# RetNet and SwiGLU on one core: the heads of a pair change places on the partitions in odd chunks, and VectorE's order around a slot changes

## The chip, the cores and the metric

The kernel runs on one core of one Trainium2 chip. The metric is the device time of one execution in microseconds; the time before is a median of three runs. All arithmetic is in fp32.

## The reference

Two parts follow one another. The first is retention in its parallel form, for 8 batches, 8 heads, 576 positions and a head size of 64. The second is a gated feed-forward layer (4608 tokens, model size 512, inner size 1536) on the result:

```python
scores = scale * np.matmul(q, k.transpose(0, 1, 3, 2))       # scale = 1/8
gamma = 1.0 - 2.0 ** (-5.0 - np.arange(H))
Dmat = np.where(rel >= 0, gamma[:, None, None] ** rel[None, :, :], 0.0)   # rel = row - column
attn = np.matmul(scores * Dmat[None], v)
x = attn.transpose(0, 2, 1, 3).reshape(B * S, H * D)
...
rms = np.sqrt(np.mean(x * x, axis=-1, keepdims=True) + 1e-06)
xn = x / rms * rms_g
g = xn @ w_gate
out = (g / (1 + np.exp(-g)) * (xn @ w_val)) @ w_out
```

## The kernel before

**Retention by chunks.** A job is one batch and one pair of heads: 32 jobs, four to a batch, so job j belongs to batch j // 4. The 576 positions are 9 chunks of 64. Within a chunk the kernel multiplies scores by a causal mask and by v; what earlier chunks contribute comes through a 64 x 64 state per head, the decayed sum of k-transposed times v over the chunks before. Row decays are folded into v ahead and into x at the end (the table gq).

The work of a job is spread over two slots, and `slot(j)` does these things in this order:

- `values(j - 1)` (L332): masked scores times v, into two PSUM banks, `av[0]` for even and `av[1]` for odd chunks.
- `scores(j)` (L270) and `states(j)` (L290): scores and chunk states of the next job, into the three banks `s` and one bank `last`.
- `weigh(j)`, on VectorE: two products `ret` (scores times mask, L303), and then the eight running sums of states (a copy at L313 and seven fused multiply-adds at L315, each of which needs the one before). The last sum reads the bank `last`.
- `carried(j - 1)`: 16 matmuls (L351) add the states' part to `av`, and four VectorE products (L366) move `av`, times gq, to `x`.

All these matmuls are 64 x 64 x 64. Each uses one quadrant of the array: the row half comes from the partitions of its inputs, the column half from those of its output. The two heads e = 0, 1 of a pair lie on partitions 0 to 63 and 64 to 127, in the inputs of `carried` (`sum`, `qT`) and in x alike; `side(e)` is that slice. A fp32 matmul leaves two records in the trace, so `carried` shows 32.

Before `carried` writes over what `values` wrote from another row half, a small GpSimd memset (`tick`, L340) that waits for `values` holds it back.

**The feed-forward layer.** A unit u is 384 tokens, 12 units. Units 0 and 1 run plainly (L536, L550), with the preparation of the weights beside them. From unit 2 on every product is made as a Strassen-like product of seven block products. `up(u, m, g)` makes one group: seven products (L479) in the order x, y, z, x, w, z, w, each 8 records on TensorE, into the banks x, y, z, w. m = 0 is the gate and m = 1 the value; three g each, so six groups i = 0 to 5 per unit. VectorE adds partial results: u2 = m1 + y and u4 = u2 + z (L486), after which the second z product may write into the bank z; results follow at L486 and L496. `across(u)` then makes the output product, again seven products of 24 records (L609), in the order x, z, w, y, x, z, w.

**The order.** It is written out by hand (`manual_schedule`): the order of the calls is the order of each engine's queue. `SLOTS` says behind which groups of a unit a slot runs. Units with u % 3 == 2 have slots behind groups 1, 3 and 5, those with u % 3 == 0 behind 0, 2, 4 and 5, those with u % 3 == 1 behind 5. So slots 10 to 12 lie in unit 2, 13 to 16 in unit 3, 17 in unit 4, and so on to slot 32 in unit 9; slots 0 to 9 are in `start()`. Of slots 9 to 32, eight (12, 16, 17, 20, 24, 25, 28, 32) are followed by `across`, the others by another group. Behind slot j follow on VectorE the transposes of q and k for the next job (L241). In unit 2 one add of w_out (`combine_out`, L580) is put between the products, as long as there are any.

The norm of the next unit is spread too: squares on ScalarE (L404) and their sums on VectorE (L410) behind group 5 (`norm_0`); the mean over the model size by three small matmuls `ms` (L422), a power on GpSimd (L428) and the diagonals (L435) behind the second product of `across` (`norm_1`); and the broadcast `rb` (L446) with the scaling of x (L448) behind the fifth (`norm_2`).

PSUM has eight banks: three for `s`, and five that serve everything else in turn; a bank is given out again once its last reader has finished.

Of the kernel before, what the change touches and what calls it, by code (L numbers as in the profile page):

```python
# [10 lines left out]
F32 = mybir.dt.float32  # L11
U32 = mybir.dt.uint32
AF = mybir.ActivationFunctionType
ALU = mybir.AluOpType
P = 128
L = P // 2


def _gamma(H):
    return 1.0 - 2.0 ** (-5.0 - np.arange(H, dtype=np.float64))  # L20


def _decay_tables(H, D):


    pairs = _gamma(H).reshape(H // 2, 2).T
    rows = np.repeat(pairs, D, axis=0)
    pos = np.arange(L)
    p = np.concatenate([pos, pos])
    t = (  # L30
        pairs.T[None] ** -p[:, None, None], rows**L,
        rows[:, :, None] ** (pos + L) / np.sqrt(D),
    )
    return [np.ascontiguousarray(x).astype(np.float32) for x in t]


def _causal_table():

    return np.ascontiguousarray(np.tile(np.triu(np.ones((L, L), np.float32)), (2, 1)))
# [3 lines left out]
def kernel(  # L43
# [11 lines left out]
    nc = tc.nc  # L55
    B, H, S, D = q.shape
    NTOK, DM = out.shape
    DFF = moe_w_gate.shape[1]
    NHP = H // 2
# [10 lines left out]
    NG = NH // 2  # L70
# [5 lines left out]
    const = ctx.enter_context(tc.tile_pool(name="const", bufs=1))  # L76
# [11 lines left out]
    def bank(name):  # L88
        return banks.tile([P, 512], F32, tag="b", name=name)
# [15 lines left out]
    top = cell("top", 255.0 * 2.0**23)  # L105
    causal = const.tile([P, L], F32, name="causal")
    gq = const.tile([P, NHP, L], F32, name="gq")
    gv = const.tile([P, NHP, 2], F32, name="gv")
    gc = const.tile([P, NHP], F32, name="gc")
    tick = const.tile([1, 1], F32, name="tick")  # L110
# [16 lines left out]
    jobs = [(b, hp) for b in range(B) for hp in range(NHP)]  # L127
    st = [{} for _ in jobs]
# [128 lines left out]
    def side(i):  # L257
        return slice(i * L, i * L + L)
# [16 lines left out]
    def state_of(d, c):  # L275

        i, odd = divmod(c, 2)
        if odd and SC + i * L == 512:
            return d["last"][:, :L]
        return d["s"][:, 1, SC + i * L : SC + i * L + L] if odd else d["s"][:, 2, i * L : i * L + L]  # L280
# [13 lines left out]

    def weigh(j):


        d = st[j]
        hp = jobs[j][1]
        s = d["s"]  # L300
        ret = d["ret"] = att.tile([P, 2, NFULL + 1, L], F32, tag="ret", name=f"ret_{j}", bufs=1)
        for e in range(2):
            nc.vector.scalar_tensor_tensor(  # L303
                out=ret[:, e], in0=s[:, e, :SC].rearrange("p (c k) -> p c k", k=L),
                scalar=float(_gamma(H)[2 * hp + e] ** -L),
                in1=causal.unsqueeze(1).to_broadcast([P, NFULL + 1, L]),
                op0=ALU.mult, op1=ALU.mult,
            )
        t = d["sum"] = att.tile([P, NC - 1, L], F32, tag="sum", name=f"sum_{j}")
        for c in range(NC - 1):  # L310
            part = state_of(d, c)
            if c == 0:
                nc.vector.tensor_copy(out=t[:, 0], in_=part)  # L313
                continue
            nc.vector.scalar_tensor_tensor(  # L315
                out=t[:, c], in0=t[:, c - 1], scalar=gc[:, hp : hp + 1], in1=part,
                op0=ALU.mult, op1=ALU.add,
            )
        del d["s"], d["last"]

    def follow(a, b):
        why = mybir.DependencyInfo(mybir.DependencyClass.Sync, mybir.DependencyReason.DATA)
        tc.add_manual_dep(a.ins, b.ins.name, why, reason="rows of the array")

    def values(j):

        d = st[j]
        av = d["av"] = [bank(f"av_{j}_{i}") for i in range(2)]
        for c in range(NC):
            i, odd = divmod(c, 2)  # L330
            for e in range(2):
                mm = nc.tensor.matmul(  # L332
                    av[odd][side(e), i * L : i * L + L],
                    lhsT=d["v"][side(odd), i, e] if c < NC - 1 else d["vt"][:, e],
                    rhs=d["ret"][side(odd), e, i],
                    start=(c < 2), stop=False, skip_group_check=True,
                )


        d["valued"] = nc.gpsimd.memset(tick, 0.0)  # L340
        follow(d["valued"], mm)

    def carried(j):

        d = st[j]
        b, hp = jobs[j]
        av = d["av"]
        for c in range(1, NC):
            i, odd = divmod(c, 2)
            for e in range(2):  # L350
                mm = nc.tensor.matmul(  # L351
                    av[odd][side(e), i * L : i * L + L], lhsT=d["sum"][side(e), c - 1],
                    rhs=d["qT"][side(e), c * L : c * L + L],
                    start=False, stop=(c >= NC - 2), skip_group_check=True,
                )
                if c == 1 and e == 0:
                    follow(mm, d["valued"])
        for c0, c1 in ((0, 2 * HU), (2 * HU, S)) if b % 2 == 0 else ((0, HU), (HU, S)):
            u, o = divmod(b * S + c0, U)
            if u not in x_of:  # L360
                x_of[u] = xp.tile([P, NHP, U], F32, tag="x", name=f"x_{u}")
            x = x_of[u][:, hp, o : o + c1 - c0].rearrange("p (c k) -> p c k", k=L)
            for first in (c0 // L, c0 // L + 1):
                i, odd = divmod(first, 2)
                n = -(-(c1 // L - first) // 2)
                nc.vector.tensor_tensor(  # L366
                    out=x[:, first - c0 // L :: 2],
                    in0=av[odd][:, i * L : (i + n) * L].rearrange("p (c k) -> p c k", k=L),
                    in1=gq[:, hp].unsqueeze(1).to_broadcast([P, n, L]), op=ALU.mult,
                )  # L370
        st[j] = {}

    def slot(j, rest=True):

        if j > len(jobs):
            return
        if rest and j > 0:
            values(j - 1)
        if j < len(jobs):
            scores(j)  # L380
            states(j)
        if j < len(jobs):
            weigh(j)
        if rest and j > 0:
            carried(j - 1)

    def prepare_next(j):
        if j + 1 < len(jobs):
            prepare(j + 1)

    def load_next(j):
        if j + 2 < len(jobs):
            load_qk(j + 2)
            load_kv(j + 2)
# [283 lines left out]
    for g in range(NG):  # L678
        for m, src in enumerate((moe_w_gate, moe_w_val)):
            for half in range(2):  # L680
                n = (half * NH + 2 * g) * P
# [13 lines left out]
    def spare(i):  # L695

        return i % 4 if i < n_up else LATER[i - n_up]
# [15 lines left out]
    def load_chunks(n, queue=nc.scalar):  # L713

        nonlocal n_loads
        while n_loads < min(n, len(chunks)) and waits_at.get(spare(n_loads)) is None:
            load_chunk(n_loads, queue)
            n_loads += 1
# [94 lines left out]
    def start():  # L813

        h_of[0] = ffn.tile([P, NF, U], F32, tag="h", name="h_0")
        tables = list(zip((causal, gv, gc, gq), (_causal_table(), *_decay_tables(H, D))))

        def table(i, queue):
            t, values_ = tables[i]
# [9 lines left out]
        for j in range(2 * NHP):  # L829
            load_first(j)  # L830
            if j == 0:
                load_tails(0, (nc.scalar, nc.scalar, nc.sync))
            elif j == 1:
                table(3, nc.sync)
            elif j == 3:
                load_tails(1, (nc.sync,) * 3)
            load_chunks((0, 0, 1, 1, 2, 2, 2, 3)[j], nc.sync)
        nc.sync.dma_start(out=rms_g, in_=moe_rms_g.rearrange("(c p) -> p c", p=P))
        load_chunks(4, nc.sync)
        turn(0)  # L840
# [3 lines left out]
        for j in range(2 * NHP):  # L844
# [7 lines left out]
            if j:  # L852
                u, c = divmod(j - 1, NHP)
# [34 lines left out]
        for u in (1, 0):  # L888
# [6 lines left out]
            if u:  # L895
                combine(1)
                slot(8, rest=False)
                following(8)
        slot(9)
        following(9)  # L900

    SLOTS = (((0, 2, 4, 5), 5), ((5,), 9), ((1, 3, 5), 10))
# [14 lines left out]
    with tc.manual_schedule():  # L919
        start()  # L920
        for u in range(2, NU):
            made = combine_out() if u == 2 else iter(())
            for i in range(2 * NG):
                for _ in up(u, i % 2, i // 2):
                    next(made, None)
                if u > 2 and i in (1, 3):
                    fetch()
                    fetch()
                if i == 2 * NG - 1:
                    rest = across(u)  # L930
                    next(rest)
                behind(u, i)
            for i, _ in enumerate(rest):
                if i == 1:
                    behind(u, 6)
                elif i == 2 and 2 * NG - 1 in SLOTS[u % 3][0]:
                    at, n = SLOTS[u % 3]
                    load_next(u // 3 * 8 + n + len(at) - 1)
                elif i == 4:
                    behind(u, 7)  # L940

# [26 lines left out]
```

## Time and profile before

| | |
|---|---|
| time, median of three runs | 1184.26 us (1182.89 to 1184.86) |
| profiled span | 1180.2 us |
| TensorE busy, matmul | 1144.4 us, 97% |
| VectorE busy | 671.1 us, 57% |
| ScalarE busy | 248.2 us, 21% |
| carried matmuls, L351 | 1024 records, 38.2 us busy |
| x products, L366 | 128 instructions, 35.5 us in all |
| sums of states, L315 | 224 instructions, 62.8 us in all |

A line of the groups by form gives source line, engine, operation, out<-in by name, the shape and the count; then the busy time, the mean of one in ns, and the idle time ahead of the group with what ended it. A line of the timeline gives start, duration, and instruction; several of a kind are merged, with their count. PEld is the weight load ahead of a matmul, and it carries the matmul's waits. Matmul records on different quadrants overlap, so their number times their duration is not their share of the span.

### The profile page before, as it was taken

What the parts mean: (1) busy time and instruction counts of PE and PEld (TensorE: products, weight loads), DVE (VectorE), ACT (ScalarE), POOL (GpSimd) and SP (SyncE); (2) the same over time, 40 slices, a digit from 0 to 9 for tenths busy, and PEclk for the clock granted to TensorE, in tenths of its full rate; (3) what the DMA queues carried; (4) which work ended last, traced back from release to release, by engine and by line L of the source; (5) the groups of instructions that cost most, each with busy time, mean ns of one, the idle gap of its engine ahead of it and who ended that gap; (6) DMA issues with size and microseconds to landing.
All of it is one profiled execution on the core that took longest, in us unless ns stands there. A gap on an engine that the chain in (4) does not pass through costs nothing.

```text
span 1180.2 us, 24260 instructions
## 1 busy us (share of the span) xinstructions
PE 1144.4 (97%) x10320; PEld 1037.0 (88%) x10320; DVE 671.1 (57%) x1362; ACT 248.2 (21%) x484; POOL 46.8 (4%) x74
## 2 busy tenths in 40 slices
PE   6789999999999999999999999999999999999998
PEld 5655555448999999999999999999999999999998
DVE  4688874118666574455664665465566555536442
ACT  5445641111211221111121120120220210120110
POOL 0000005400000000000000000000000000000000
PEclk9899999999999999999999999999999999999999
DMA  9744312322954536126335446306525502403304
GB/s 223 205 112 146 139 72 58 125 66 41 264 134 66 164 96 138 62 72 122 101 94 94 110 117 137 117 17 123 132 64 133 157 5 85 130 1 94 121 1 108
DMA packets 282220, 125.24 MB, mean 106 GB/s; under 512 B 257152, under 2 KB 264704, under 8 KB 282112
## 3 DMA queue, kind: packets, MB, share of 16 engines
q1 hardware_dynamic: 271440, 108.32, 36.4%
q10 hardware_dynamic: 10672, 15.38, 3.9%
q8 instruction: 81, 1.33, 0.5%
q14 instruction: 27, 0.22, 0.1%
HBM read 108.70 MB, written 14.94 MB: 105 GB/s over the span
## 4 chain that ended last, share of the span: by engine, by line
PE 85%; DVE 10%; DMA 2%; ACT 2%; issue 1%; SPq 0%; DVEq 0%; POOL 0%; POOLq 0%; ACTq 0%
PE x L479 13%; PE z L479 13%; PE w L479 13%; PE up L536 8%; PE wo L609 7%; PE y L479 7%; PE out L550 5%; PE xo L609 4%; PE zo L609 4%; PE yo L609 3%; DVE sum L315 2%; PE av L351 2%; PE av L332 1%; PE s L270 1%; DVE sq L410 1%
## 5 line engine op out<-in xcount | busy, mean ns | idle before, releaser
L503 ACT COPY m<-x 128x384 f32<-128x384 f32 x60 | 28.7, 478 | 430.9 <-PE x L479 430.9
L479 PE MATMUL z<-x,w_gate 128*128 128x192 f32 x480 | 87.9, 326 | 2.2 <-DVE sum L315 2.2
L479 PE MATMUL x<-x,w_val 128*128 128x192 f32 x480 | 89.8, 331 | 0.0
L479 PE MATMUL x<-x,w_gate 128*128 128x192 f32 x480 | 88.6, 328 | 0.0
L479 PE MATMUL w<-sums,w_gate 128*128 128x192 f32 x480 | 87.8, 326 | 0.0
L479 PE MATMUL z<-x,w_val 128*128 128x192 f32 x480 | 87.8, 326 | 0.0
L479 PE MATMUL w<-sums,w_val 128*128 128x192 f32 x480 | 87.8, 326 | 0.0
L609 PE MATMUL xo<-h,w_out 128*128 128x192 f32 x480 | 82.1, 328 | 0.0
L609 PE MATMUL wo<-h,w_out 128*128 128x192 f32 x480 | 82.0, 328 | 0.0
L479 PEld LDWEIGHTS z<-x,w_gate 128*128 128x128 f32 x480 | 79.6, 190 | 2.5 <-DVE sum L315 2.5
L479 PEld LDWEIGHTS x<-x,w_val 128*128 128x128 f32 x480 | 80.0, 192 | 0.6
L479 PEld LDWEIGHTS x<-x,w_gate 128*128 128x128 f32 x480 | 79.3, 190 | 0.5
L479 PEld LDWEIGHTS w<-sums,w_val 128*128 128x128 f32 x480 | 79.7, 190 | 0.0
L479 PEld LDWEIGHTS w<-sums,w_gate 128*128 128x128 f32 x480 | 79.7, 190 | 0.0
L479 PEld LDWEIGHTS z<-x,w_val 128*128 128x128 f32 x480 | 79.6, 190 | 0.0
L609 PEld LDWEIGHTS xo<-h,w_out 128*128 128x128 f32 x480 | 78.1, 190 | 0.5
L609 PEld LDWEIGHTS wo<-h,w_out 128*128 128x128 f32 x480 | 78.1, 190 | 0.0
L486 DVE TENSOR_TENSOR u<-m,y 128x384 f32<-128x384 f32 x60 | 32.8, 546 | 79.4 <-PE y L479 79.4
L486 DVE TENSOR_TENSOR h<-u,w 128x384 f32<-128x384 f32 x60 | 33.3, 555 | 73.7 <-PE w L479 73.7
L303 DVE SCALAR_TENSOR_TENSOR ret<-s,causal 128x320 f32<-128x320 f32 x64 | 28.4, 485 | 67.0 <-PE last L290 42.2
L498 ACT ACTIVATE h<-h 128x384 f32<-128x384 f32 x90 | 47.0, 523 | 88.6 <-DVE h L486 88.6
L536 PE MATMUL up<-x,w_val 128*128 128x384 f32 x192 | 62.7, 487 | 2.1 <-ACT w_val L544 2.1
(150 smaller groups left out, 1783.0 us busy)
## 6 DMA issues: line engine op xcount, KB each, us to landing
w_out<-w_blocks SPq DMA_DIRECT2D x70, 768.0 KB, 5.1
out_dram<-o SPq DMA_DIRECT2D x304, 24.0 KB, 1.6
qraw<-in_q_dram SPq DMA_DIRECT2D x96, 72.0 KB, 2.6
kraw<-in_k_dram SPq DMA_DIRECT2D x96, 72.0 KB, 2.6
k<-in_k_dram SPq DMA_DIRECT2D x48, 128.0 KB, 2.9
v<-in_v_dram SPq DMA_DIRECT2D x48, 128.0 KB, 2.8
w_blocks<-w_out SPq DMA_DIRECT2D x7, 768.0 KB, 7.0
w_out<-in_moe_w_gate_dram ACTq DMA_DIRECT2D x4, 1024.0 KB, 5.2
```

The lines of the kernel that those rows point to most:

```text
L270: nc.tensor.matmul(s[side(odd), e, i * L : i * L + L], lhsT=d["kT"][side(e), c * L : c * L + L], rhs=d["qT"][side(e), c * L : c * L + L], ...
L303: nc.vector.scalar_tensor_tensor(out=ret[:, e], in0=s[:, e, :SC].rearrange("p (c k) -> p c k", k=L), scalar=float(_gamma(H)[2 * hp + e] ** ...
L315: nc.vector.scalar_tensor_tensor(out=t[:, c], in0=t[:, c - 1], scalar=gc[:, hp : hp + 1], in1=part, op0=ALU.mult, op1=ALU.add,)
L332: mm = nc.tensor.matmul(av[odd][side(e), i * L : i * L + L], lhsT=d["v"][side(odd), i, e] if c < NC - 1 else d["vt"][:, e], rhs=d["ret"][s ...
L351: mm = nc.tensor.matmul(av[odd][side(e), i * L : i * L + L], lhsT=d["sum"][side(e), c - 1], rhs=d["qT"][side(e), c * L : c * L + L], start ...
L479: nc.tensor.matmul(ps[:, i * HU : i * HU + HU], lhsT=w_up[m][:, 2 * blk + c, cut], rhs=t_of[u][blk][:, c], start=(start and i == c == 0), ...
L486: nc.vector.tensor_tensor(out=o, in0=a, in1=pairs_of(ps), op=ALU.add)
L498: nc.scalar.activation(out=o, in_=c, func=AF.Silu)
L503: nc.scalar.copy(out=s1, in_=pairs_of(x_))
L536: nc.tensor.matmul(ps[:, :U], lhsT=w_up[m][:, 4 * half + c, i * P : i * P + P], rhs=x_of[u][:, c], start=(c == 0), stop=(c == NHP - 1),)
L550: nc.tensor.matmul(ps[:, :DM], lhsT=h_of[u][:, f, s * P : s * P + P], rhs=w_out[:, f], start=(f == 0), stop=(f == NF - 1),)
L609: nc.tensor.matmul(ps[:, i * HU : i * HU + HU], lhsT=w_slots[:, k % 4, c, i * P : i * P + P], rhs=rhs[:, c], start=(start and i == c == 0) ...
```

## The change

It has three parts.

1. *Exchange.* From job 8 on, the products of odd chunks write head e to the other half of the partitions, in `values` and in `carried`. In `carried`, even chunks then use two quadrants of the array and odd chunks the other two. The last VectorE products bring the heads back to their places: each product of an odd chunk becomes two of 64 partitions, which read one half and write the other. They need the decay table with its halves exchanged, gx, which is loaded ahead of rms_g.
2. *x ahead of the sums.* The sums of states leave `weigh` and become `sums(j)`. From slot 8 on they run after `carried(j - 1)`, so the x products come first on VectorE.
3. *ms later.* The mean of squares, the power and the diagonals go behind the third product of `across` instead of the second.

```diff
+    gq = rows[:, :, None] ** (pos + L) / np.sqrt(D)
+    t = pairs.T[None] ** -p[:, None, None], rows**L, gq, np.roll(gq, D, axis=0)
...
+    gx = const.tile([P, NHP, L], F32, name="gx")
...
+    def column(j, odd, e):
+        return side(1 - e if odd and j >= 2 * NHP else e)
...
-                    av[odd][side(e), i * L : i * L + L],
+                    av[odd][column(j, odd, e), i * L : i * L + L],
...
-                nc.vector.tensor_tensor(
-                    out=x[:, first - c0 // L :: 2],
-                    in0=av[odd][:, i * L : (i + n) * L].rearrange("p (c k) -> p c k", k=L),
-                    in1=gq[:, hp].unsqueeze(1).to_broadcast([P, n, L]), op=ALU.mult,
-                )
+                moves = [(slice(0, P),) * 2]
+                if column(j, odd, 0) != side(0):
+                    moves = [(side(e), column(j, odd, e)) for e in range(2)]
+                for to, at in moves:
+                    g = (gq if to == at else gx)[at, hp].unsqueeze(1)
+                    nc.vector.tensor_tensor(
+                        out=x[to, first - c0 // L :: 2],
+                        in0=av[odd][at, i * L : (i + n) * L].rearrange("p (c k) -> p c k", k=L),
+                        in1=g.to_broadcast([at.stop - at.start, n, L]), op=ALU.mult,
+                    )
...
             weigh(j)
+        if j < 2 * NHP:
+            sums(j)
         if rest and j > 0:
             carried(j - 1)
+        if 2 * NHP <= j < len(jobs):
+            sums(j)
...
+        table(4, nc.sync)
         nc.sync.dma_start(out=rms_g, in_=moe_rms_g.rearrange("(c p) -> p c", p=P))
...
             for i, _ in enumerate(rest):
-                if i == 1:
+                if i == 2:
                     behind(u, 6)
-                elif i == 2 and 2 * NG - 1 in SLOTS[u % 3][0]:
                     at, n = SLOTS[u % 3]
-                    load_next(u // 3 * 8 + n + len(at) - 1)
+                    if 2 * NG - 1 in at:
+                        load_next(u // 3 * 8 + n + len(at) - 1)
                 elif i == 4:
                     behind(u, 7)
```

## The prediction

> **What bounds the kernel now.** I read the page's busy times first, then TensorE's waits, then the chain of waits around one slot, then the timeline of that slot, and last the groups by form for the operation that is split.
>
> ```profile
> PE 1144.4 (97%) x10320; PEld 1037.0 (88%) x10320; DVE 671.1 (57%) x1362; ACT 248.2 (21%) x484; POOL 46.8 (4%) x74
> ```
>
> TensorE is busy for 97% of the span, so there are two ways to gain: shorter TensorE work, or fewer TensorE waits. The waits that the change aims at are small (total us, times, longest us):
>
> ```profile
> PE ms L422 <- DVE sq L410: 3.3, 7, 0.5
> ...
> PE z L479 <- DVE sum L315: 2.2, 1, 2.2
> ```
>
> The chain of waits through a slot inside unit 3 (start, us, work) shows what each part of a slot costs TensorE:
>
> ```profile
> 371.13 0.67 PE av L332 x34
> ...
> 371.86 0.53 PE s L270 x36
> ...
> 372.44 0.34 PE s L290 x22
> ...
> 372.90 0.93 PE av L351 x32
> 373.83 1.50 PE x L479 x8
> ```
>
> Per record, scores take 0.53/36 = 14.7 ns and states 0.34/22 = 15.5 ns, but the carried products 0.93/32 = 29 ns. All are 64 x 64 x 64. Scores, states and values visit four quadrants of the array (two row halves, two column halves); `carried` visits only the two where row half and column half agree. The factor is two, as is the number of quadrants.
>
> The timeline behind that slot (start, us, instruction) shows how closely VectorE follows:
>
> ```profile
> 373.76 0.21 DVE L313 COPY sum<-s 128x64 f32<-128x64 f32 x1
> ...
> 374.01 1.86 DVE L315 SCALAR_TENSOR_TENSOR sum<-sum,gc,s 128x64 f32<-128x64 f32 x6
> ...
> 375.98 0.28 DVE L315 SCALAR_TENSOR_TENSOR sum<-sum,gc,last 128x64 f32<-128x64 f32 x1
> 376.18 0.94 DVE L366 TENSOR_TENSOR x<-av,gq 128x128 f32<-128x128 f32 x4
> 376.31 1.32 PEld L479 LDWEIGHTS z<-x,w_val 128*128 128x128 f32 x8
> ...
> 377.04 0.77 DVE L241 STREAM_TRANSPOSE qT<-qraw 128x576 f32<-128x576 f32 x1
> ...
> 377.73 0.73 DVE L241 STREAM_TRANSPOSE kT<-kraw 128x576 f32<-128x576 f32 x1
> ...
> 378.39 0.52 DVE L486 TENSOR_TENSOR u<-m,y 128x384 f32<-128x384 f32 x1
> ...
> 379.01 0.55 DVE L486 TENSOR_TENSOR u<-u,z 128x384 f32<-128x384 f32 x1
> ...
> 380.20 1.33 PEld L479 LDWEIGHTS z<-x,w_val 128*128 128x128 f32 x8
> ```
>
> Two margins count. The first z product takes the bank that the last sum frees: that sum ends at 376.26 and z's weights start at 376.31, so the margin is the 0.05 us of a handover. The second z product needs u4 (the add `u<-u,z`), which ends at 379.56; its weights start at 380.20, a margin of 0.64. The slots of units 2, 3, 5, 6, 8 and 9 that lie between two groups repeat these two numbers, with four exceptions: in slots 9 and 10 the second margin is only 0.12 and 0.17, because adds of w_out stand in between; slot 31 has no transposes behind it; slot 30 was held up by a TensorE pause of 1.65 us at 944.6.
>
> ```profile
> L366 DVE TENSOR_TENSOR x<-av,gq 128x192 f32<-128x192 f32 x64 | 19.6, 349 | 0.0
> L366 DVE TENSOR_TENSOR x<-av,gq 128x128 f32<-128x128 f32 x32 | 9.0, 283 | 0.6 <-PE av L351 0.6
> L366 DVE TENSOR_TENSOR x<-av,gq 128x64 f32<-128x64 f32 x32 | 6.9, 215 | 0.0
> ```
>
> A job's four x products last 2 x 349 + 283 + 215 = 1196 ns, but from the first start to the next work they take 377.04 - 376.18 = 0.86 us: each overlaps its successor by (1.196 - 0.86)/4 = 0.084 us.
>
> **What the Trainium skill says.** TensorEngine Tiling (Array Packing), Key Properties: different tiles can load weights and multiply in parallel. The trace agrees (15 against 29 ns). PSUM — Partial Sum Buffer, section on bank collisions: writes from different row tiles must not meet in one bank and quadrant. The exchange respects this: within `carried` each half of each bank is written from one row half only, as before. TensorE: Matmul & The Clock Gate, the part on the array's architecture: VectorE's queue is strict first in, first out, so order decides; every VectorE instruction above starts in program order. VectorE: DVE Perf Modes, section "Two Vector instructions with no wait between them": an instruction whose start quadrant differs from that of the last read or write in that memory is held until all earlier ones have finished. The trace before has no VectorE operation that moves between partition halves, so no run here shows it yet.
>
> **The change, part by part.**
>
> *Exchange, on TensorE.* Odd chunks now use the two idle quadrants, so four follow one another. At the rate of scores and states (14.7 ns) a job's 32 records take 0.47 instead of 0.93: 0.46 us less in each of 24 jobs (8 to 31), 11.0 us of TensorE work. `values` visits four quadrants before and after: no change.
>
> *Exchange, on VectorE.* The two odd x products per job become four of 64 partitions each. Length, not partitions, sets their time (I assume the same duration by form), so a 64- and a 192-element product are added: by spacing 0.13 + 0.26 = 0.39 us. One saving: the last sum now needs no separate wait on `last` (its gap is 0.11 after 375.87, against 0.03 between the others), -0.07. That is the cheap bound, +0.32. If the moves are held, the overlaps go too. In an even batch (192; 192 twice; 128; 64 twice) the six products take 349 x 3 + 283 + 215 x 2 = 1760 ns, and the sums' copy is held as well: 1.76 - 0.86 - 0.07 = +0.83. In an odd batch the last is an even chunk and overlaps by 0.08: +0.75. I take the held values, since the page's rule fits these operations literally; +0.32 stays as the other end.
>
> *x ahead of the sums.* The first z and w products now wait for x products, not for the last sum. These end at about 373.76 + 1.4 = 375.2, before z's new natural start 376.31 - 0.46 = 375.85: no wait, and w comes later still. But sums, both transposes, u2 and u4 queue behind x on VectorE, and the second z product waits for u4. That chain starts at the end of the states, which the change doesn't move, so it ends later by the added VectorE time.
>
> *Slots between two groups.* The second z product therefore starts later by (added time - margin + 0.05). Odd batches, eight slots (13 to 15, 21 to 23, 29, 30): 0.75 - 0.59 = +0.16 each, +1.3. Even batches, five slots (11, 18, 19, 26, 27): 0.83 - 0.59 = +0.24, +1.2. Slot 9: 0.83 - 0.07 = +0.76; slot 10: 0.83 - 0.12 = +0.71. Slot 31, without transposes, keeps -0.46. Sum +3.5 us: here the 0.46 saved by the exchange is waited away, and the 2.2 us wait of slot 9 moves to u4.
>
> *Slots ahead of `across`* (12, 16, 17, 20, 24, 25, 28, 32). No z waits here, and the next use of VectorE's results is loose: the block that the fourth product needs ends at 342.10 and the product starts at 345.46. So 8 x 0.46 = 3.7 us stay.
>
> *ms one product later.* The sums of squares end at 340.83 and with +0.8 at 341.6; ms now follows the third product, near 344. The seven waits, 3.3 us, go. Behind ms queue r, the power on GpSimd and the diagonals, 343.82 - 341.77 = 2.1 us, and rb comes two products of 3.9 us later: hidden. The load of the table gx (128 KB, like one k load, which lands 2.9 us after its issue) stands behind the first jobs' loads, ahead of weights used tens of us later: nothing.
>
> Sum: +3.5 - 3.7 - 3.3 = -3.5 us, so 1184.26 - 3.5 = **1180.8 us**.
>
> **Rivals.**
> - *Four quadrants, moves not held.* For: the rule is not shown here. Added +0.32: 13 slots gain 0.59 - 0.32 = 0.27 (3.5), slots 9 and 10 lose 0.25 and 0.20, slot 31 gains 0.46; with 7.0 from `across` 10.5 less: 1173.8.
> - *No gain in the array*: two row halves alternate in one bank, or the order of quadrants matters. Against: pairs already do so at 29 ns, two at a time. Held: slots between groups lose 4.0 (without slot 31's gain), ms gives 3.3: 1185.0.
> - *Slower.* Either the moved products cost twice their duration (another 2 x 349 + 2 x 215 ns = 1.13 us per job, x 15 slots = 17 on 1180.8: 1198), or the array stays at 29 ns and each of some six holds costs 0.1 more (15 x 0.6 = 9 on 1185.0): 1194. Against: a product's time by form follows its length, and nothing shows such a penalty.
>
> **How the numbers follow.** Held and four quadrants 0.60; not held 0.22; no array gain 0.10; slower 0.08. The first case is uncertain by some 2 us (another 0.03 us per hold costs 15 x 0.17 = 2.5), so seven tenths of it end below 1181.9, which is 0.2% under the time before, and the rest within 0.2%. The case of no array gain I split 0.02, 0.05 and 0.03 over faster, same and slower. Faster 0.42 + 0.22 + 0.02 = 0.66; same 0.18 + 0.05 = 0.23; slower 0.08 + 0.03 = 0.11. The range 1172.5 to 1186.0 takes in the second and third cases.
>
> **What would show it.** Carried products: 0.47 us in the chain instead of 0.93. TensorE waits of z on u4 (L504 after) in some 15 slots, 0.5 to 0.7 us each; no ms wait on sq. x products: if held, six in 1.7 us, else 1.25. I am wrong if carried stays at 0.93, if z's waits on u4 are near 0.2 (not held), or if z waits on x products.

## The result, and the profile after

| | before | after |
|---|---|---|
| median | 1183.58 us (4 runs, 1182.10 to 1184.86) | 1175.24 us (4 runs, 1171.12 to 1176.68) |
| ratio | | 0.9924 [0.9896, 0.9952] |
| profiled span | 1180.2 us | 1173.6 us |

The change makes the kernel 8.3 us faster, where 3.5 were predicted; 1175.24 lies inside the range. First line: the page's busy times after.

```profile
PE 1134.3 (97%) x10320; PEld 1024.2 (87%) x10320; DVE 692.0 (59%) x1410; ACT 248.7 (21%) x484; POOL 46.4 (4%) x74
```

TensorE's busy time fell by 10.1 us (from 1144.4), VectorE's rose by 20.9 (from 671.1). The span fell by 6.6, less than TensorE's work, so TensorE is idle for longer than before. TensorE's waits after (total us, times, longest us):

```profile
PE z L497 <- DVE u L504: 8.6, 15, 1.6
...
PE z L497 <- DVE x L380: 1.2, 1, 1.2
```

All seven waits of `ms` on sq are gone, and 15 waits of the second z product on u4 have come. The chain of waits around slot 12, which `across` follows, shows the carried products (start, us, work):

```profile
334.57 0.47 PE av L360 x31
335.04 2.96 PE xo L627 x17
```

0.47 us instead of 0.93: the four quadrants do run at the rate of the scores. The timeline behind slot 13, which another group follows, shows where that gain goes (start, us, instruction; in brackets the idle time ahead and what ended it):

```profile
375.13 1.27 PEld L497 LDWEIGHTS x<-x,w_val 128*128 128x128 f32 x8
...
375.59 0.28 DVE L380 TENSOR_TENSOR x<-av,gq 128x128 f32<-128x128 f32 x1
375.88 1.20 DVE L380 TENSOR_TENSOR x<-av,gx 64x64 f32<-64x64 f32 x4
...
377.11 0.36 DVE L380 TENSOR_TENSOR x<-av,gq 128x192 f32<-128x192 f32 x1
377.38 0.21 DVE L317 COPY sum<-s 128x64 f32<-128x64 f32 x1
377.63 1.86 DVE L319 SCALAR_TENSOR_TENSOR sum<-sum,gc,s 128x64 f32<-128x64 f32 x6
377.67 1.33 PEld L497 LDWEIGHTS z<-x,w_val 128*128 128x128 f32 x8
...
381.08 0.52 DVE L504 TENSOR_TENSOR u<-m,y 128x384 f32<-128x384 f32 x1
381.70 0.56 DVE L504 TENSOR_TENSOR u<-u,z 128x384 f32<-128x384 f32 x1
...
382.31 1.27 PEld L497 LDWEIGHTS z<-x,w_val 128*128 128x128 f32 x8 [0.71 <-DVE u L504]
```

The six x products take 377.38 - 375.59 = 1.79 us, against 0.86 for the four before. The four moving ones follow one another without overlap: the four durations (226, 217, 360 and 352 ns) and the gaps of about 0.01 us between them make up the 1.20 us of the merged line. In the groups by form (last: busy, mean ns of one, idle before) half the partitions take as long as all did:

```profile
L380 DVE TENSOR_TENSOR x<-av,gx 64x192 f32<-64x192 f32 x48 | 17.0, 355 | 0.7
...
L380 DVE TENSOR_TENSOR x<-av,gx 64x64 f32<-64x64 f32 x48 | 10.6, 222 | 0.9
```

Before, the same lengths took 349 and 215 ns. In the timeline, the first z product starts at 377.67 with no wait; the second waits for u4, which ends at 382.26; its weights start 0.05 later.

The clearest view of the whole is a table of stretches: from the end of one slot's carried products to the end of the next slot's, in us, as the records of TensorE give them. Slots of one kind repeat to 0.01 us, so effects of 0.1 us can be read, which the timed runs can't do. The time up to slot 9's end is left out: between two profiles of one and the same order (e5 and e11 below) it differed by 7.3 us. Of that time e11 spent 20.5 us at half clock and e5 3.4, which is enough for the whole difference.

| stretch into slot | before | after |
|---|---|---|
| 10; 11 | 23.73; 21.10 | 24.60; 21.92 |
| 12, 19, 20, 27, 28 (behind an even batch's slot) | 21.10 | 21.44 |
| 14, 15, 22, 23 (behind an odd batch's slot) | 21.10 | 21.32 |
| 16, 24 | 12.00 | 12.23 |
| 13, 21, 29 (17, 18, 25, 26 alike), with one `across` each | 41.33 | 40.16 |
| 30; 31 | 22.96; 22.78 | 21.32; 21.32 |
| 32 | 11.45 | 11.00 |
| from slot 9 to the end | 913.6 | 906.5 |

So the 7.1 us are: -8.2 in seven stretches with an output product, -3.5 + 0.4 in 30 and 31, and +4.2 in the rest. The -3.5 was not in the prediction. The profile before has this in slot 30 (timeline):

```profile
943.76 0.71 PEld L351 LDWEIGHTS av<-qT,sum 64*64 64x64 f32 x20
...
946.25 0.43 PEld L351 LDWEIGHTS av<-qT,sum 64*64 64x64 f32 x12 [1.78 <-issue]
...
946.75 2.10 PEld L479 LDWEIGHTS x<-x,w_val 128*128 128x128 f32 x8
```

and in the table by windows (window, length, busy us of each engine, granted clock, DMA share, GB/s):

```profile
947.10:950.50 3.40, 3.40 (x13) 3.40 (x12) 2.49 (x7) 0.48 (x1) 0.00 (x0) 0.50 0.02 5
```

TensorE stops for 1.8 us in the middle of the carried products, waiting for nothing that the profile names ("issue"), and the next 3.4 us run at half the clock, which costs another 1.7. Neither is in the profile after, where all 32 weight loads of slot 30's carried products run in one piece:

```profile
941.47 0.60 PEld L360 LDWEIGHTS av<-qT,sum 64*64 64x64 f32 x32
```

### The profile page after: what moved, and what is told of

It reads as the page before. It is cut to its first block, busy times and chain, and to the rows that moved or that the text cites. A ratio compares the mean times of both kernels' runs of the same rounds, so it can differ in the third digit from the quotient of the medians.

```text
span 1173.6 us, 24291 instructions
## 1 busy us (share of the span) xinstructions
PE 1134.3 (97%) x10320; PEld 1024.2 (87%) x10320; DVE 692.0 (59%) x1410; ACT 248.7 (21%) x484; POOL 46.4 (4%) x74
## 3 DMA queue, kind: packets, MB, share of 16 engines
q8 instruction: 81, 1.33, 0.5%
## 4 chain that ended last, share of the span: by engine, by line
PE 83%; DVE 12%; issue 2%; DMA 2%; ACT 1%; DVEq 0%; SPq 0%; POOL 0%; POOLq 0%; ACTq 0%
PE z L497 12%; PE w L497 12%; PE x L497 10%; PE up L554 8%; PE xo L627 7%; PE wo L627 7%; PE zo L627 7%; PE out L568 5%; PE y L497 5%; PE yo L627 3%; DVE sum L319 3%; DVE x L380 2%; PE av L341 2%; PE s L270 2%; PE s L290 1%
```

## The experiments

Times are medians with ratios to the kernel before on the same chip. "From slot 9" is the profiled time from the end of slot 9's carried products to the end of the program (913.6 before, 906.5 after). A profile is of one of the timed executions; those of e2 and e5 are 2.9 and 7.7 us faster than the medians of their kernels, and what the median execution lost there was not traced.

### The change again

> The changed kernel once more, for its time and for a second profile. Theory: 8 us less than before, of which the trace of slots explains 4 to 5; the rest is a pause of TensorE at 944 us in the profile before (1.8 us, and 1.7 us more at half clock behind it) that the changed kernel doesn't have. If the pause belongs to the program, this profile has none at that place either; if it comes by chance, pauses turn up in some profiles of either kernel and the time spreads by some 4 us.

1175.06 us, ratio 0.9936 [0.9920, 0.9952], and 906.9 from slot 9. The stretches agree with the first profile to 0.05 us, but for slot 30 (0.3 longer: the 32 weight loads of its carried products take 0.90 us instead of 0.60, with a short pause where the kernel before pauses).

### Each part alone

e1 is the exchange alone: the sums again ahead of `carried`, `ms` again behind the second product of `across`. e2 is x ahead of the sums alone, e3 is ms later alone:

```diff
# e1, against after
-        if j < 2 * NHP:
+        if j < len(jobs):
             sums(j)
         if rest and j > 0:
             carried(j - 1)
-        if 2 * NHP <= j < len(jobs):
-            sums(j)
...
-                if i == 2:
+                if i == 1:
                     behind(u, 6)
...
# e2, against after: the same for ms, and
-        return side(1 - e if odd and j >= 2 * NHP else e)
+        return side(e)
# e3, against before
-                if i == 1:
+                if i == 2:
                     behind(u, 6)
...
```

> The exchange alone: sums of states ahead of the x products, ms behind the second product as before. Theory (the chain on VectorE decides): the carried products still shrink from 0.93 to 0.47 us, but z starts when the last sum ends, as before, and everything on VectorE behind the sums comes 0.83 to 0.9 us later. So u4 makes the second z product wait 0.7 us more in some 13 slots between groups, and ms waits 0.47 + 0.46 + 0.85 = 1.8 us in seven units instead of 0.5. Sum: about +5 us from the slots between groups and +6 from the seven units, so 1194 where before is 1183.6. Rival (the exchange is worth its TensorE work, 11 us, wherever it stands): 1173.

> x ahead of the sums alone, no exchange, ms as before. Theory: the z product no longer waits for the last sum, but TensorE arrives there at the same time as before, and u4 and the squares stand behind the same sum of VectorE work; only the wait of 2.2 us in slot 9 moves to u4. So -0.5 us, within 0.3% of before: 1183. Rival (x products earlier free banks and squares, which is where the gain comes from): 2 to 5 us less, 1179 to 1181.

> ms behind the third product alone. Theory: the seven waits go. TensorE's matmul row counts them as 3.3 us, its weight loads as 5.2 us (0.74 each), because the weights of ms could not be loaded ahead while it waited. So -3.3 us if the matmul row is right, -5.2 us if the weight loads count: 1180.3 or 1178.4 where before is 1183.6. Rival: the wait moves to rb or to the first product of the next unit, and nothing is gained.

| | median | ratio | from slot 9 |
|---|---|---|---|
| e1, exchange | 1208.37 us | 1.0210 [1.0183, 1.0238] | 940.6 |
| e2, x ahead | 1180.45 us | 0.9977 [0.9965, 0.9988] | 909.7 |
| e3, ms later | 1179.31 us | 0.9967 [0.9956, 0.9978] | 907.2 |

e3: the stretches with an `across` fall from 41.33 to 40.62: the wait was worth 0.71 each, 5.0 in seven, not 3.3. TensorE's waits of the kernel before show why, once those of the weight loads (PEld; below, the weight row, where PE is the matmul row) are asked for too:

```profile
PEld ms L422 <- PE zo L609: 5.2, 7, 0.7
```

In the matmul row the same seven waits stand at 3.3. The weights of `ms` are the sums of squares themselves, so their load can't be done ahead, and TensorE does nothing while it runs; the matmul row sees only the part ahead of it. (The releaser in that line is only the event that came last.) The other 1.4 us of e3's gain lie in slots 30 and 31: it has a pause of 2.0 us there, but no half clock behind it.

e2: the slots don't move (21.10; slot 10 0.19 shorter), the `ms` waits shrink by 0.06. Its gain is that slots 30 and 31 take 21.10 each: no pause.

e1 is far slower than expected. VectorE's sums of squares now come after the sums and the held x products, and `ms` waits longer:

```profile
PE ms L438 <- DVE sq L426: 13.6, 7, 2.0
```

What comes on top of these waits is in the windows around the first of them:

```profile
344.00:347.00 3.00, 1.31 (x9) 1.01 (x7) 2.79 (x5) 0.06 (x1) 0.00 (x0) 1.00 0.50 162
...
348.80:352.20 3.40, 3.40 (x13) 3.40 (x12) 0.68 (x3) 0.00 (x0) 0.64 (x1) 0.50 0.03 13
```

After each of the seven waits (2.1 to 2.3 us in the weight row) TensorE runs at half its clock for 3.4 us, after one of them for 6.8. A period of 3.4 us costs 1.7. With it a stretch adds up: longer wait 2.2 - 0.74 = 1.5, half clock 1.7, exchange -0.46, together 2.7; measured 44.08 - 41.33 = 2.75. So the exchange without the other two parts loses 27 us from slot 9 on, some 20 of them in the seven stretches with an `across`.

### The moves on VectorE

e4 leaves out the moving back: the x products take 128 partitions as before, and the heads of odd chunks stay exchanged in x.

```diff
-                if column(j, odd, 0) != side(0):
+                if False:
                     moves = [(side(e), column(j, odd, e)) for e in range(2)]
```

> This kernel is the changed one with its x products left as they were before the change: each takes all 128 partitions, so the heads of odd chunks stay exchanged in x (the moving back is left out, and the output with it). If the moves on VectorE are what makes the second z product wait for u4, the chain through u4 is as short as before, its margin of 0.64 us holds the 0.46 us saved by the exchange, and 13 slots go from +0.22 or +0.34 to -0.46; slots 9 and 10, with margins of 0.12 and 0.17, go from +0.86 and +0.82 to about -0.15 and -0.2. Together 11.4 us less than the changed kernel: about 1163.7. z waits on u4 all but vanish. If it is the order (x before the sums) and not the moves that causes the waits, the time stays near 1175.

1166.93 us, ratio 0.9855 [0.9833, 0.9877]; from slot 9 895.0, which is 11.5 less than after. Slots between groups take 20.64 us (21.10 - 0.46), and one wait on u4 is left (1.2 us, in slot 9). So the moves make the waits, not the order.

e5 keeps the moves, and sorts a job's products by the half that they write:

```diff
                 for to, at in moves:
...
+                    rank = 0 if to == at else 1 + to.start
+                    pieces.append((rank, x[to, first - c0 // L :: 2], odd, to, at, i, n))
+        for _, o, odd, to, at, i, n in sorted(pieces, key=lambda t: t[0]):
...
```

> The changed kernel, with a job's x products sorted: both even chunks' products first, then those that write partitions 0 to 63, then those that write 64 to 127. The arithmetic is the same. If an instruction is held only where the start partition changes, three of six holds go: the x stretch falls from 1.79 us by 3 x 0.084 = 0.25 to about 1.54, each wait on u4 by the same, and 15 slots gain 3.8 us: about 1171.3. If instead each product that moves between halves is slow in itself, or each is held whatever went before, the stretch stays at 1.79 and the time at 1175.

The timeline of VectorE behind slot 13 in e5:

```profile
372.04 0.54 DVE L384 TENSOR_TENSOR x<-av,gq 128x128 f32<-128x128 f32 x2
372.62 1.00 DVE L384 TENSOR_TENSOR x<-av,gx 64x64 f32<-64x64 f32 x4
373.64 0.23 DVE L317 COPY sum<-s 128x64 f32<-128x64 f32 x1
```

1.60 us instead of 1.79. Two moves that write the same half overlap again, by 0.08 us; at each change of half the next one waits. In this odd batch sorting takes the holds from five to three, in an even batch from six to three; the stretches fall by 0.18 and 0.30 (both to 21.14), so 0.09 to 0.10 us for a hold. My expectation took three off for both. The size of the products isn't the cause, since the same six run.

The time, though, is 1178.47 us, ratio 0.9958 [0.9936, 0.9979], no better than after. The profiled execution was the fastest of the ten (1170.82 us); from slot 9 it has 906.3. Twelve stretches gain 2.9 us, and three things give it back: a pause of 1.85 us in slot 30, as before the change; the second wait in slot 9 grows from 1.94 to 2.48 us, as the first one shrinks from 1.49 to 0.64; and behind that wait the half clock sets in, with the stretch into slot 10 at 25.98 instead of 24.60.

### Later sums

e6 leaves the changed kernel's x products, and puts sums, transposes and the next loads of 12 slots behind the last product of the group after:

```diff
-            slot(j)
-            prepare_next(j)
...
+            wait = i + 1 < 2 * NG and i + 1 not in at and j < len(jobs)
+            slot(j, later=wait)
+            if wait:
+                due.append(j)
...
-                for _ in up(u, i % 2, i // 2):
+                for n, _ in enumerate(up(u, i % 2, i // 2)):
                     next(made, None)
+                    if n == 6:
+                        overdue()
```

> The changed kernel, but in the 12 slots that are followed by two groups (10, 11, 13, 14, 18, 19, 21, 22, 26, 27, 29, 30) the sums of states, the transposes and the next loads come behind the last product of the group after the slot, so on VectorE they queue behind that group's u2 and u4. If the wait is only a matter of what is queued ahead of u4, it goes in these slots: 1.28 us in slot 10, 0.80 in each of five, 0.68 in each of six, 9.4 us in all: about 1165.8, with three waits on u4 left (slots 9, 15, 23). If the moved work only meets the next group's adds instead, waits of the same size come one group later and the time stays near 1175.

1167.27 us, ratio 0.9864 [0.9842, 0.9885], the fastest of all that compute the whole; from slot 9 900.0. The 12 waits on u4 are gone (stretches of 20.64), 9.4 us as expected. Given back are 2.9 us: 0.8 and 1.1 in the stretches into slots 16 and 24, 0.9 into slot 13. TensorE's waits name the first two:

```profile
PE x L497 <- ACT m L521: 2.8, 2, 1.5
```

The timeline ahead of slot 16 shows a new chain:

```profile
418.17 0.35 ACT L250 ACTIVATE vt<-vt,gv 64x64 f32<-64x64 f32 x1 [2.31 <-DMA vt<-in_v_dram]
...
419.06 0.46 ACT L521 COPY m<-x 128x384 f32<-128x384 f32 x1
...
419.57 1.27 PEld L497 LDWEIGHTS x<-x,w_val 128*128 128x128 f32 x8 [1.51 <-ACT m L521]
```

The loads start later with the transposes, ScalarE waits for them in its queue, and the copy of m1 that frees the bank x waits behind.

e10 is e6 with slots 14 and 22 in the changed kernel's order:

```diff
-            wait = i + 1 < 2 * NG and i + 1 not in at and j < len(jobs)
+            wait = i + 1 < 2 * NG and i + 1 not in at and j not in (14, 22) and j < len(jobs)
```

> The kernel with the later sums, but slots 14 and 22 keep the changed kernel's order. With the later sums their loads come a group later, ScalarE waits for them with a scaling of v, and the copy of m1 behind it holds the next x product for 1.5 to 1.8 us after slots 15 and 23. If that is the chain, these two waits go (stretches into slots 16 and 24 fall from 13.02 and 13.35 to 12.2), and two waits of z on u4 of 0.7 us come back: about 0.7 us less in all, span 1165.3 beside 1166.0, time about 1166.5. If the x waits have another cause, they stay and the time is 1.4 us longer.

The waits on the copy are gone and the stretches into 16 and 24 are 12.22 and 12.23, those into 15 and 23 21.33 and 21.32: the chain is as read. From slot 9 899.5, 0.5 less than e6. 1168.85 us, ratio 0.9895 [0.9872, 0.9918]: the intervals overlap, so the timed runs don't tell it from e6.

e7 has e5's sorting and e6's later sums:

> The sorted x products and the later sums together. Only slots 9, 15 and 23 still have the waits that sorting shortens, so after the later sums it brings 3 x 0.25 = 0.75 us more: about 1165.0. If sorting is worth 3.8 us by itself for another reason than the waits on u4 (shorter VectorE work in every slot), the two add up: about 1162.

1170.63 us, ratio 0.9890 [0.9866, 0.9914]; from slot 9 899.9, level with e6. The sorting brings 0.7, 0.4 and 0.6 in the stretches into slots 16, 24 and 13, and loses 1.4 in slot 10, with the same half clock behind a wait of 2.48 us. The gains don't add up.

### The change without the exchange

```diff
-        return side(1 - e if odd and j >= 2 * NHP else e)
+        return side(e)
```

> The changed kernel without the exchange: x ahead of the sums and ms later remain. From the stretches between the ends of carried in the runs so far: the exchange saves 0.46 us in each of seven stretches with an output product (3.2 us) and costs 4.9 us in the slots between groups (waits of the second z product on u4). If the three parts simply add, this kernel is 1.7 us faster than the changed one: span 1171.9 against 1173.6 and 1172.3, time about 1173.5; stretches between groups 21.10 us, stretches with an output product 40.62 us (40.16 with the exchange). If the exchange is what makes the change pay, the time is above 1178.

1175.08 us, ratio 0.9942 [0.9923, 0.9961]; from slot 9 904.9, that is 1.7 and 2.0 less than the two profiles of after. Slots between groups take 21.10, stretches with `across` 40.62, as expected. In the chain around slot 12 the carried products take what they took before:

```profile
332.41 0.93 PE av L360 x32
333.34 4.10 PE xo L627 x24
```

And of the waits on u4 only slot 9's remains:

```profile
PE z L497 <- DVE u L504: 1.2, 1, 1.2
```

So the exchange, as the change places it, gains nothing: 3.2 us in `across`, paid for with 4.9 in the slots. In the timed runs the two kernels are level.

### The pause

e9 is the kernel before, and e11 is e5, with the first two loads of w_out in unit 9 called two groups later:

```diff
-                if u > 2 and i in (1, 3):
+                if u > 2 and i in ((1, 3) if u != 9 else (3,)):
+                    if u == 9:
+                        fetch()
+                        fetch()
```

> The kernel before, with one edit: in unit 9 the two loads of w_out that are issued behind group 1 come behind group 3, two groups later. In the profile before, TensorE pauses for 1.7 us within the carried products of slot 30 (at 944.3) while a block of its instructions is still being loaded; those loads of w_out fill the DMA engines from 935 to 944. If the late instruction block is the cause, and the busy DMA engines make it late, the pause and the 3.4 us at half clock behind it go: the stretches into slots 30 and 31 fall from 22.96 and 22.78 to 21.10 us, 3.5 us together, time about 1179.8 beside 1183.3. If the pause has another cause (something in the carried products themselves), it stays: no change.

> The kernel with the sorted x products and the same edit of the w_out loads in unit 9. Its profile had the pause of 1.85 us at 935.8, and its timed runs a lower granted clock than its profiled one. If the late instruction block causes the pause, the stretch into slot 30 falls from 22.98 to 21.14 us, and the time from about 1178 by 2 to 4 us. If the pause stays, the loads are not its cause. If the pause goes and the low clock of most runs stays (near 0.989), the half-clock periods come from elsewhere.

The edit missed: slot 30 has no job left to load for, so nothing stands between the two places in SyncE's queue, and the loads start where they did (12.1 us ahead of the end of slot 30's carried products in e9, 11.9 before). Both count as repeats of known orders. e9: 1183.58 us, ratio 1.0007 [0.9993, 1.0022], pause of 1.94 us, no half clock behind it, but one behind slot 9's wait of 2.53. e11: 1177.83 us, ratio 0.9953 [0.9939, 0.9967], pause of 2.6 us.

What the 14 profiles do show: the pause stands always behind the same instruction of TensorE, the 17,599th (counted in order of their starts: weight loads, matmuls and the waits of its sequencer); two pauses early in the program stand behind the 1,727th (in 13 profiles), which is 62 x 256 earlier, and the 1,472nd (in all 14), 255 before that. The page lists a DMA queue "instruction" with 81 packets and 1.33 MB, 16 KB each. In the six profiles with the long pause (before, e1, e3, e5, e9, e11) TensorE goes on 2.2 to 2.5 us after one such packet starts; after the two early pauses it does so 2.3 to 3.4 us after one. In the other eight the packet starts 2.4 us or more before TensorE gets there. In the kernel after it is 2.4: it arrives just in time. All four profiles without x ahead (three orders) have the pause. Of the ten profiles with it, only those of the sorted products without later sums (two) have it. That the missing block of instructions makes the pause is strongly suggested. Why the packet starts late is open: DMA engines full of w_out are a suspect that no run here tested. They don't suffice alone: in the profile after, the packet starts at 939.30, in time, and the engines are fully busy then too (DMA share 1.01 from 938 to 940).

## Why the prediction was right, and where not

**Side and mechanisms.** Faster was right. Of what was to be seen, all came: carried at 0.47 us; z waiting on u4 in 15 slots, 0.71 to 0.84 us each in the weight row (predicted: 0.5 to 0.7; slots 9 and 10 more: 1.94 and 1.30); no `ms` wait; six x products in 1.79 us (predicted: 1.7). One of the signs of being wrong came too, in one place: in slot 9, z waits on the x products.

**Exchange on TensorE.** 0.46 us a job: right.

**Held moves.** Right, and now shown: e4 without moves has no waits, e5 with fewer changes of half has shorter ones. The Trainium skill, VectorE: DVE Perf Modes, section "Two Vector instructions with no wait between them", says that an instruction with another start quadrant than the last access waits for all earlier ones to finish; this case's traces agree, at 0.09 to 0.10 us for each.

**Slots between groups.** The term was small by 1.2 us: +0.22, +0.34, +0.87 and +0.82 where +0.16, +0.24, +0.76 and +0.71 were worked out. Holds were priced as the lost overlap of 0.084 alone; the gaps of 0.01 to 0.03 us between held instructions come on top. The 2.2 us wait of slot 9 did not move to u4 as a whole: z waits for x (1.2) and then for u4. The working had the x products over 1.4 us after their start, where its own held price is 1.76. Between groups the conclusion, no wait, still holds, with 0.2 us to spare in slot 13 (377.46 to 377.67).

**Slots ahead of `across`.** Right: 40.62 to 40.16.

**ms.** Mis-sized: 3.3 us from the matmul row, 5.0 measured. The step that was too small is "the seven waits, 3.3 us, go". The wait should have been read in the weight row.

**Slot 30.** That "slot 30 was held up by a TensorE pause of 1.65 us" was seen, and taken as given in both kernels. It was not: pause and half clock, 3.5 us in the profile, are gone with the new order.

In sum, from slot 9 on: predicted -3.0 (the -3.5 without the 0.46 of slot 9's own carried products); slots +1.2, ms -1.7 and slot 30 -3.5 on top give -7.0, and -7.1 was measured. The first two nearly cancel, so the size of the miss is the pause, a term that the prediction put at nothing. By parts, from the stretches of e3, e8 and after: ms later -5.0, pause and half clock -3.5, x ahead by itself -0.2, exchange +1.6. So the side was right because of `ms` and the pause: the exchange, put at -0.2 (+3.5 in the slots, -3.7 ahead of `across`), cost time in the profiles. That 1175.24 still lies in the range is in part luck, for the range reached so far down to take in "moves not held".

**Rivals.** "Moves not held" forecast 1173.8, closer to the time than mine, for a reason that e5 rules out: the holds are there. "No gain in the array" falls with 0.47. "Slower" by a double price of moves falls with the 217 and 360 ns of the moving products, the same as before by length.

## What to carry to other kernels

Before work is moved from TensorE to VectorE, ask what on TensorE waits behind VectorE's queue: here the 0.46 us saved in a slot became a wait of 0.7, and paid only once the queued sums went behind the next group (e6: 8 us better than the change, and from slot 9 on 4.9 less than e8, which has no exchange; later sums without the exchange were not run). Sort VectorE work by the partition half that it writes, so that fewer instructions are held; here a hold cost 0.09 to 0.10 us, too little to show in the timed runs of e5. Read a wait of TensorE in the weight-load row: where the weights are what is waited for, the matmul row shows only part of it.

## What the hardware showed that was not expected

- **Half clock after short waits.** In e1 each of seven waits of 2.1 to 2.3 us, in an otherwise dense stream, was followed by 3.4 us (once 6.8) at half clock. The seven waits of 0.74 us before never were, nor those of 1.94 in four profiles of after's x order; a wait of 2.48 was in three of three; the wait of 2.53 us in slot 9 was in one of four profiles (e9; not before, e1, e3). The Trainium skill, TensorE: Matmul & The Clock Gate, section "What's actually happening", gives an idle window of about 3.4 us, free-running, as the condition. The length of the periods agrees; that 2 us of waiting suffice does not. The kept traces also show why waits of one length differ. In each of the 14 profiles all changes of the clock but those at the program's ends lie on a grid of 3.413 us, to 2 ns, and the half clock goes with how busy TensorE was within one window of that grid. From 70 us on, all 11 windows in which its matmul records cover less than 41% are followed by half clock, and 9 of the 22 with 41 to 52%. Of those with more only one is, and it runs at half clock itself (in e1's period of 6.8 us). Slot 9's wait of 2.53 us lies inside one window in e9 (41% busy); in the first profile a border cuts it (47%). What decides between 41 and 52% is open.
- **Pauses for a block of instructions**, 1.8 to 2.8 us, at one fixed place in TensorE's instructions, and gone or back with small changes of order elsewhere.
